# Threshold attention and a tanh-shrink layer pair: scores one slot further ahead, one slot more before the weights, and a v load in three parts

## The chip, the cores and the metric

The kernel runs on one core of one Trainium2 chip. The time is the device time of an execution in microseconds. Of the kernel before there are three executions: 511.3, 513.72 and 514.99 us, so its median is 513.72 us. One further execution was profiled: it took 509.47 us, and the span between its first and last recorded instruction is 507.7 us.

## The reference

Eight batches of eight heads have 576 rows of 64 numbers for q, k and v. What is computed is an attention that keeps only scores near the maximum of their row, followed by two dense layers:

```python
scores = scale * np.matmul(q, k.transpose(0, 1, 3, 2))
thresh = np.max(scores, axis=-1, keepdims=True) - tau
scores = np.where(scores >= thresh, scores, -1000000000.0)
attn = np.exp(scores - np.max(scores, axis=-1, keepdims=True))
attn = attn / (np.sum(attn, axis=-1, keepdims=True) + 1e-09)
x = np.matmul(attn, v)            # then heads side by side: 4608 x 512
h = x @ w_in                      # w_in 512 x 2048
g = h - np.tanh(h)
out = g @ w_out                   # w_out 2048 x 512
```

## The kernel before, in words

**Tiles.** Two heads form a pair; there are 32 pairs, four to a batch. A pair has nine score tiles of 128 query rows by 576 keys: four for each head, and a ninth ("shared") that holds the last 64 rows of both. So there are 288 tiles. Tiles go in twos, A (even number) and B (odd).

**Slots.** The order is written out by hand. One loop over a slot number `s` (L820) issues in each slot one tile's step of every stage:

- `scores(s + AHEAD)` (L373): matmuls of turned q against turned k, hi and lo halves (`kT` and a half-swapped copy `kS`), into PSUM; then VectorE copies the scores out and takes the row's maximum (L406). `AHEAD` is 8. The two shared tiles between an even and an odd pair are scored in one slot, and the slot before that scores none.
- `kink` of tile `s + MASK` (L425): ScalarE masks the scores into `z` (L433). `MASK` is 5. For pairs from 6 on, SyncE then issues a DMA that transposes a `z` of two tiles into `zT` (L440); for earlier pairs TensorE does this.
- `weights` of tile `s` (L442): ScalarE takes the exponential, from `zT` (L469) for pairs from 6 on. For the first 36 tiles this is done four slots earlier (L815).
- `attend` of tile `s - LAG` (L474): TensorE multiplies the weights with v. `LAG` is 2. `norm` divides on VectorE, and `emit_x` (L537) transposes a finished pair into the layers' input.

**Layers.** After each batch of attention a block of layer steps is started (L822 to L824), and a string of 36 letters per block (`PATTERN`, L622) says in which of the next 36 slots an "h" step (`hidden`, four matmuls of 512 columns, L565) or a "y" step (`project`, a quarter of an output tile, L591) is issued. `bend` puts tanh on ScalarE (L578), `shrink` the subtraction on VectorE (L584). What is left after the last tile runs as a tail.

**Preparation.** `plan` (from L743) lists for each pair at how many slots ahead of its first score it is loaded, split and turned. Pairs from 8 on: the loads (`load_part`, L143) are issued from ScalarE's queue, k in one DMA, q in two, v in two (128 KB and 160 KB). GpSimd splits k and q into hi and lo halves (`split`, L225 to L229), SyncE issues a transposing DMA for each (`turn`, L301), GpSimd makes `kS` from `kT` in two copies (`swap`, L323) and casts v (`split_v`, L258 to L263). The slots are the numbers in `LATER` (L746): "k0", "q0", "q1", "v0", "v1" are load parts, "ks", "qs", "vs" splits, "kt", "qt" turns, "kw" the swap. Pairs 1 to 7 take theirs from `PREP` and `k_lead`. The tags of turned k, q and kS have two buffers each (`qk_pool`, L114).

**Queues.** Each engine works in program order. ScalarE's queue holds the loads of pairs from 8 on between its activations; SyncE's queue holds all transposing DMAs and the output stores. In the built program every DMA of both queues signals one of eight completion semaphores, taken in turn, and is issued only when the DMA eight places before it, which used the same one, is complete.

```python
        at = i - 4 if i < HPAIR * TPP else i
        atts.setdefault(at + LAG, []).append(i)
        if i < NTILE:
            wts.setdefault(at, []).append(i)
            kinks.setdefault(i // 2 * 2 + 2 - AHEAD if i < 4 else i - MASK, []).append(i)
```

Of the kernel before, what the change touches and what calls it, by code (L numbers as in the profile page):

```python
# [9 lines left out]
F32 = mybir.dt.float32  # L10
# [8 lines left out]
def kernel(  # L19
# [12 lines left out]
    P = 128  # L32

    B, H, S, D = q.shape
# [11 lines left out]
    HPAIR = H // 2  # L46
# [5 lines left out]
    TPP = 9  # L52
# [7 lines left out]

    W = 2 * S

    AHEAD = 8
    LDK = 16
    MASK = 5
    LAG = 2


# [30 lines left out]
    for i in range(6):  # L99
# [8 lines left out]
    pool = lambda name, bufs, **kw: ctx.enter_context(  # L108
        tc.tile_pool(name=name, bufs=bufs, **kw)
    )  # L110
    PSUM = bass.MemoryType.PSUM
    raw_pool = pool("raw", 2)
    hl_pool = pool("hl", 2)
    qk_pool = pool("qk", 2)  # L114
    sc_pool = pool("sc", AHEAD - MASK + 2)
    st_pool = pool("st", 12)
    z_pool = pool("z", 4)
# [16 lines left out]
    raws = {}  # L134
    DUAL = 8
    AT_ONCE = 1
    LOADER = nc.scalar

    boths = {}

    def load_part(p, t, part):  # L143


        b, h0 = p // HPAIR, 2 * (p % HPAIR)
        if part == 0:
            both = raw_pool.tile([P, 2, 10, D], F32, name=f"{t}raw", tag=t)
            both = boths[t] = both[:, 0:AT_ONCE, :, :]
            for a in range(AT_ONCE):  # L150
                raws[p + a, t] = both[:, a, :, :]
        both = boths[t]
        rows = {"k": k, "q": q, "v": v}[t][b, h0 : h0 + 2 * AT_ONCE, :, :]
        heads = both.rearrange("p a (h c) d -> p (a h) (c d)", h=2)
        if t == "k":
            dst = both[:, :, 0:TPP, :].rearrange("p a c d -> p a (c d)")
            rows = rows.rearrange("(a h) s d -> a (h s) d", h=2).rearrange(
                "a (p c) d -> p a (c d)", c=TPP
            )
        elif t == "v":  # L160
            rows = rows.rearrange("h (p c) d -> p h (c d)", c=TPP)
            if part == 0:
                dst, rows = heads[0:64, :, 0 : 4 * D], rows[:, :, 0 : 4 * D]
            else:
                dst, rows = heads[64:P, :, :], rows[:, :, 4 * D :]
        elif part == 0:
            dst = heads[:, :, 0 : 4 * D]
            rows = rows[:, 0:512, :].rearrange("h (p c) d -> p h (c d)", c=4)
        else:
            dst = both[:, part - 1, 4, :]  # L170
            rows = rows[2 * part - 2 : 2 * part, 512:S, :].rearrange("h s d -> s h d")
        LOADER.dma_start(out=dst, in_=rows)

    def load(p, t):
        b, h0 = p // HPAIR, 2 * (p % HPAIR)
        hs = slice(h0, h0 + 2)
        src = {"k": k, "q": q, "v": v}[t]
        eng = nc.sync
        r = raw_pool.tile([P, 2, 10, D], F32, name=f"{t}raw", tag=t)[:, 0, :, :]
        raws[p, t] = r  # L180
        eng.dma_start(
            out=r.rearrange("p (h c) d -> p h (c d)", h=2)[:, :, 0 : 4 * D],
            in_=src[b, hs, 0:512, :].rearrange("h (p c) d -> p h (c d)", c=4),
        )
        rem = src[b, hs, 512:S, :].rearrange("h s d -> s h d")
        if t == "v":
            eng.dma_start(out=r[0:64, 4:10:5, :], in_=rem)
        else:
            eng.dma_start(out=r[:, 4, :], in_=rem)

    def load_first(t, h, eng):

        src = {"k": k, "q": q}[t]
        if (0, t) not in raws:
            raws[0, t] = raw_pool.tile([P, 2, 10, D], F32, name=f"{t}raw", tag=t)[:, 0, :, :]
        r = raws[0, t]
        if h is None:
            rem = src[0, 0:2, 512:S, :].rearrange("h s d -> s h d")
            eng.dma_start(out=r[:, 4, :], in_=rem)
        else:  # L200
            eng.dma_start(
                out=r[:, 5 * h : 5 * h + 4, :].rearrange("p c d -> p (c d)"),
                in_=src[0, h, 0:512, :].rearrange("(p c) d -> p (c d)", c=4),
            )
# [72 lines left out]
    def turn_chunk(out, c, lhsT, mixed=True):  # L277
        rhs = ident_f16
        if c == 4 and mixed:
            out, rhs = in_heads(out), by_head(rhs)  # L280
        nc.tensor.matmul(
            out=out, lhsT=lhsT, rhs=rhs, is_transpose=True, start=True, stop=True
        )

    def k_lead(p):
        if p < HPAIR + 2:
            return 6 if p in (2, 4) or p == HPAIR + 1 else 5 - (p == 1)
        return (6, 6)[1 - p % 2]
# [29 lines left out]
    def swap(p):  # L318
        m = mats[p, "k"]
        sw = qk_tile("ks")  # L320
        for lo, hi in ((0, D), (D, 0)):
            o, i = sw[lo : lo + D, 0:W], m[hi : hi + D, 0:W]
            nc.gpsimd.tensor_copy(out=o, in_=i)  # L323
        mats[p, "ks"] = sw
# [264 lines left out]
    def project(m, ms, part, ps, last, cols=slice(0, d_model)):  # L589
# [31 lines left out]

    PATTERN = lambda m: {  # L622
        0: '-h--h-hh--h-hh-h-hh-h--hh-h--hh-y-yy',
        B - 2: 'hyhyhyhyhyhyhyhyhyhyhyhyhyhyhyhy',
    }.get(m, 'h-yhyhhyhyyhyyhh-yhhyhhy-yhyyh-yyhhy')

    FIRST = 3
    quarters = lambda m: [(m, ms, part) for ms in range(4) for part in range(4)]
# [90 lines left out]
    def w_load(piece):  # L719
# [6 lines left out]
        else:  # L726
# [18 lines left out]

    LATER = {  # L746
        0: (
            ("k0", 17), ("q0", 15), ("v0", 13), ("kt", 7), ("q1", 15),
            ("ks", 8), ("v1", 12), ("vs", 6), ("qs", 10), ("qt", 7),
            ("kw", 3),  # L750
        ),
        1: (
            ("k0", 19), ("v1", 14), ("q0", 18), ("v0", 16), ("qs", 11),
            ("q1", 17), ("qt", 8), ("ks", 13), ("vs", 6), ("kt", 10),
            ("kw", 7),
        ),
    }
    for p in range(DUAL, NPAIR):
        first = TPP * p - AHEAD
        at = lambda d, f: plan.setdefault(first - d, []).append(f)  # L760
        for what, d in LATER[p % 2]:
            t, w = what
            f = {
                "0": lambda p=p, t=t: load_part(p, t, 0),
                "1": lambda p=p, t=t: load_part(p, t, 1),
                "2": lambda p=p, t=t: load_part(p, t, 2),
                "s": lambda p=p, t=t: split_v(p) if t == "v" else split(p, t),
                "t": lambda p=p, t=t: turn(p, t),
                "w": lambda p=p, t=t: swap(p) if k_by_dma(p) else None,
            }[w]  # L770
            at(d, f)
    for p in range(1, DUAL):
        first = TPP * p - AHEAD
        for d, f in PREP[3 if p == 1 else 0 :]:
            d -= p == 1 and d == 3
            if p > HPAIR and d >= LDK - 2:
                d = ((16, 14, 12), (17, 15, 13))[1 - p % 2][LDK - d]
            elif d in (7, 8) and q_by_dma(p):
                d = ((9, 9) if d == 7 else (10, 10))[1 - p % 2]
            elif d == 4:  # L780
                d = 4
            elif d == 5:
                d = k_lead(p)
            elif p in (2, 4):
                d = {8: 9, 7: 8}.get(d, d)
            plan.setdefault(first - d, []).append(lambda p=p, f=f: f(p))
        d = (6, 7)[1 - p % 2] if q_by_dma(p) else 3 - (p == 1 or p >= 5)
        d = 4 if p in (2, 4) else d
        plan.setdefault(first - d, []).append(lambda p=p: turn(p, "q"))

    load(0, "v")
# [8 lines left out]
        load(1, t)  # L800
    pieces = w_pieces()
    load_when = [3, 8, 13, 18, 21, 25, 29, 34, 38, 42, 46, 49, 52, 55, 58, 61]
    cast_when = [11, 19, 27] + [4 * i + 32 for i in range(3)] + [3 * i + 44 for i in range(10)]

    todo, stage = [], 0
    fold = const.tile([P, 64], BF16, name="fold")
# [1 line left out]
    for at in sorted(plan):  # L808
        if at < -AHEAD:
            plan.setdefault(-AHEAD, []).extend(plan.pop(at))  # L810


    kinks, wts, atts = {}, {}, {}
    for i in range(NTILE + 3):
        at = i - 4 if i < HPAIR * TPP else i  # L815
        atts.setdefault(at + LAG, []).append(i)
        if i < NTILE:
            wts.setdefault(at, []).append(i)
            kinks.setdefault(i // 2 * 2 + 2 - AHEAD if i < 4 else i - MASK, []).append(i)
    for s in range(-AHEAD, NTILE + LAG + 3):  # L820
        p, j = divmod(max(s, 0), TPP)
# [43 lines left out]
                emit_x(pp - 1)  # L865
        for step in plan.pop(s, []):
            step()
        if s + AHEAD in cast_when:
            w_cast()
        if s + AHEAD in load_when:  # L870
            w_load(next(pieces))

    for _, step in todo:
# [16 lines left out]
    _ = bass_utils  # L890
# [35 lines left out]
```

## Time and profile before

| what | value |
|---|---|
| median of three executions | 513.72 us (511.3 to 514.99) |
| profiled execution, and its span | 509.47 us, 507.7 us |
| TensorE (PE) busy | 484.1 us, 95% |
| ScalarE (ACT) busy | 432.7 us, 85% |
| VectorE (DVE) busy | 400.0 us, 79% |
| GpSimd (POOL) busy | 291.1 us, 57% |
| DMA | 95.61 MB, mean 188 GB/s |

Busy time is a sum over the span, and the stages differ: attention alone at first, then attention with layers, then layers alone from about 437 us. So the stretches matter more than the totals. "L396" names a line of the kernel; "kS<-kT" a tile written from a tile; ACTq and SPq are the queues of ScalarE and SyncE, where a DMA is issued. A wait line reads: engine, its line, who released it, total us, times, longest.

### The profile page before, as it was taken

The page shows a single profiled execution, that of the slowest core. Times are in us where ns is not written, and L with a number is a line of the kernel's source. Part 1 is how long each engine was busy: PE and PEld are TensorE (multiplying, and loading weights), DVE is VectorE, ACT ScalarE, POOL GpSimd, SP SyncE. Part 2 cuts the span into 40 slices and gives each one's busy share as a digit, 9 for nine tenths or more (in the row PEclk, how much of TensorE's full clock was granted, in tenths as well). Part 3 has the DMA queues.
Part 4 walks back from the last instruction along what each step waited for, and adds up shares of the span by engine and source line. Part 5 has one row for each costly group of instructions (what it writes and reads, how often), then busy time and mean ns, then how long its engine had stood idle before and what let it go on. Part 6 is the DMA issues. An engine that isn't in the chain of part 4 may idle for free.

```text
span 507.7 us, 12146 instructions
## 1 busy us (share of the span) xinstructions
PE 484.1 (95%) x4274; PEld 270.4 (53%) x4336; DVE 400.0 (79%) x1149; ACT 432.7 (85%) x617; POOL 291.1 (57%) x390
## 2 busy tenths in 40 slices
PE   8999899888999999999999999999998999999997
PEld 4667566444555555555555555555554555544444
DVE  5899979976989898988898889889887887544440
ACT  5999999988999999999999999999998999533430
POOL 7999999967676657574757575575567500000000
PEclk9999999998999999999999999999999999999999
DMA  6852658999999999999999999999999976211013
GB/s 198 264 163 90 196 176 220 226 189 220 211 245 228 242 227 223 242 249 211 228 228 268 216 228 228 223 231 231 212 220 252 197 131 113 76 41 43 24 40 83
DMA packets 234525, 95.61 MB, mean 188 GB/s; under 512 B 205152, under 2 KB 223840, under 8 KB 234464
## 3 DMA queue, kind: packets, MB, share of 16 engines
q1 hardware_dynamic: 213520, 73.17, 74.7%
q10 hardware_dynamic: 20944, 21.67, 15.7%
q8 instruction: 34, 0.56, 0.5%
q14 instruction: 27, 0.22, 0.1%
HBM read 36.70 MB, written 9.44 MB: 91 GB/s over the span
## 4 chain that ended last, share of the span: by engine, by line
PE 61%; POOL 12%; DMA 10%; ACT 6%; issue 5%; DVE 3%; ACTq 1%; SPq 0%; POOLq 0%
PE psY L591 20%; PE psH L565 16%; PE psS L396 14%; PE psO L499 4%; DMA zT<-z 3%; POOL kS L323 3%; PE psHt L565 3%; ACT pT L469 3%; ACT z L433 2%; DMA kT<-khl 2%; DMA kraw<-in_k_dram 2%; PE psS L387 2%; ACT th L578 1%; POOL w_in_sb L717 1%; DMA qraw<-in_q_dram 1%
## 5 line engine op out<-in xcount | busy, mean ns | idle before, releaser
L406 DVE TENSOR_SCALAR_CACHE_REDUCE sc<-psS 128x576 f32<-128x576 f32 x288 | 213.2, 752 | 28.7 <-PE psS L396 14.2
L433 ACT ACTIVATE z<-sc,nb 128x576 bf16<-128x576 f32 x288 | 217.2, 770 | 13.5 <-DVE nb L418 9.4
L591 PE MATMUL psY<-w_out_sb,g 128*128 128x512 bf16 (+1 forms) x564 | 141.5, 375 | 1.7 <-DVE nb L418 0.2
L469 ACT ACTIVATE pT<-zT 128x1152 f16<-128x1152 bf16 x117 | 135.0, 1154 | 4.6 <-DMA zT<-z 4.6
L565 PE MATMUL psH<-xT,w_in_sb 128*128 128x512 bf16 x448 | 118.8, 379 | 5.3 <-DVE g L584 2.2
L323 POOL COPY kS<-kT 64x1152 f16<-64x1152 f16 x62 | 70.7, 1141 | 74.6 <-DMA kT<-khl 55.2
L584 DVE SCALAR_TENSOR_TENSOR g<-th,psH 128x512 bf16<-128x512 f32 x128 | 87.6, 684 | 28.9 <-ACT th L578 28.1
L396 PE MATMUL psS<-kT,qT 128*128 128x512 f16 (+1 forms) x512 | 104.8, 286 | 3.3 <-DVE sc L406 1.5
L396 PE MATMUL psS<-kS,qT 128*128 128x512 f16 (+1 forms) x512 | 104.9, 287 | 0.1
L396 PEld LDWEIGHTS <-qT 128*128 128x128 f16 x1024 | 72.8, 98 | 58.6 <-issue 4.2
L578 ACT ACTIVATE th<-psH 128x512 f32<-128x512 f32 x128 | 74.6, 583 | 20.9 <-PE psH L565 20.9
L591 PEld LDWEIGHTS <-g 128*128 128x128 bf16 x592 | 51.3, 98 | 55.1 <-issue 1.1
L565 PEld LDWEIGHTS <-w_in_sb 128*128 128x128 bf16 x576 | 49.0, 98 | 57.3 <-issue 5.5
L499 PE MATMUL psO<-vb,pT 128*128 128x65 bf16 x1024 | 53.6, 195 | 0.0
L499 PEld LDWEIGHTS <-pT 128*128 128x128 f16 x1024 | 44.5, 98 | 9.9
L229 POOL TENSOR_TENSOR qhl<-qraw,qhl 128x576 f16<-128x576 f32 x31 | 39.7, 1281 | 2.6
L229 POOL TENSOR_TENSOR khl<-kraw,khl 128x576 f16<-128x576 f32 x31 | 39.7, 1280 | 2.6
L461 ACT ACTIVATE pT<-psZ 128x512 f16<-128x512 bf16 (+1 forms) x54 | 35.1, 653 | 2.5 <-PE psZ L452 2.3
L225 POOL TENSOR_SCALAR qraw<-qraw 128x576 f32<-128x576 f32 x31 | 20.8, 670 | 20.9 <-DMA qraw<-in_q_dram 19.6
L603 DVE COPY yo<-psY 128x512 f32<-128x512 f32 (+1 forms) x31 | 21.1, 680 | 13.3 <-PE psY L591 12.4
L492 PE MATMUL psO<-vb,pT 128*128 128x130 bf16 x128 | 28.3, 221 | 2.1 <-ACT pT L469 1.8
L525 DVE TENSOR_TENSOR osb<-psO,rc 128x256 bf16<-128x256 f32 x64 | 27.2, 425 | 2.2
(77 smaller groups left out, 448.6 us busy)
## 6 DMA issues: line engine op xcount, KB each, us to landing
out_dram<-yo SPq DMA_DIRECT2D x32, 256.0 KB, 2.9
kraw<-in_k_dram ACTq DMA_DIRECT2D x24, 288.0 KB, 4.2
qraw<-in_q_dram ACTq DMA_DIRECT2D x24, 256.0 KB, 4.1
wt<-in_moe_w_in_dram SPq DMA_DIRECT2D x8, 512.0 KB, 4.6
wt<-in_moe_w_out_dram SPq DMA_DIRECT2D x8, 512.0 KB, 4.2
vraw<-in_v_dram ACTq DMA_DIRECT2D x24, 160.0 KB, 4.0
vraw<-in_v_dram ACTq DMA_DIRECT2D x24, 128.0 KB, 4.2
vraw<-in_v_dram SPq DMA_DIRECT2D x8, 256.0 KB, 3.6
```

The source lines that it names most:

```text
L229: nc.gpsimd.tensor_tensor(out=hl[:, :, 1, :], in0=x, in1=hl[:, :, 0, :], op=ALU.subtract)
L323: nc.gpsimd.tensor_copy(out=o, in_=i)
L396: nc.tensor.matmul(out=ps[:, dst], lhsT=lhs, rhs=cols(p, kk, hh), start=(n == 0), stop=(n == 1),)
L406: nc.vector.tensor_scalar(out=sc, in0=ps[:, lo : lo + S], scalar1=SC, scalar2=None, op0=ALU.mult, op1=ALU.max, accum_out=mx[:, c : c + 1],)
L433: nc.scalar.activation(out=z, in_=sc, func=ACT.Prelu, bias=nb, scale=1.0, alpha=STEEP)
L461: nc.scalar.activation(out=pt[:, off * P : (off + n) * P], in_=ps[:, 0 : n * P], func=ACT.Exp)
L469: nc.scalar.activation(out=pt[:, 0 : n * P], in_=zts.pop(i)[:, 0:n, :], func=ACT.Exp)
L499: nc.tensor.matmul(out=po[:, t - 1 + ab, :], lhsT=pt[:, blk * P : (blk + 1) * P], rhs=vb[:, hh, c, :], start=False, stop=(n == 7), skip_gr ...
L565: nc.tensor.matmul(out=ps, lhsT=w_in_sb[:, c, n * P : (n + 1) * P], rhs=xs[m][:, c, :] if m < B else xR[:, c, :, :], start=(c == 0), stop= ...
L578: nc.scalar.activation(out=th, in_=ps, func=ACT.Tanh)
L584: nc.vector.scalar_tensor_tensor(out=gs[m][:, n, :], in0=th, scalar=-1.0, in1=ps, op0=ALU.mult, op1=ALU.add,)
L591: nc.tensor.matmul(out=ps, lhsT=gs[m][:, n, ms * P : (ms + 1) * P], rhs=w_out_sb[:, n, cols], start=(n == 0), stop=(n == DF_C - 1),)
```

## The change

`AHEAD` becomes 9 and `MASK` 6: scores and mask of a tile are issued one slot earlier against its weights. The table `SOONER` moves weights and attend of the tiles of pairs 0 to 3 five slots forward instead of four, and of pairs 4 and 5 one slot instead of none, so that for pairs 0 to 5 the distance from score to mask, weights and attend is what it was. From pair 6 on, mask and weights stand six slots apart instead of five. Attend follows the weights by two slots as before.

`qk_pool` gets three buffers. The v load becomes three DMAs, 128, 128 and 32 KB, from ScalarE's queue (24 more DMAs in all). `LATER` has other slots; pairs 8 and 9 have tables of their own. `LEADS` lists the slots of pairs 1 to 7; against the first score of the pair they are the former ones, but for pair 5, whose k is turned one slot later. Two layer patterns change: the one of the second block, and the one used where none is named. Blocks begin at the same slot as before, which is now one score later. `raw_pool` tiles lose a half that was never used. `cast_when` is the same list written out.

```diff
-    AHEAD = 8
+    AHEAD = 9
     LDK = 16
-    MASK = 5
+    MASK = 6
...
-    qk_pool = pool("qk", 2)
+    qk_pool = pool("qk", 3)
...
+    V_PARTS = ((0, 0, 4), (64, 4, 8), (64, 8, 9))
...
-            both = raw_pool.tile([P, 2, 10, D], F32, name=f"{t}raw", tag=t)
-            both = boths[t] = both[:, 0:AT_ONCE, :, :]
+            both = raw_pool.tile([P, AT_ONCE, 10, D], F32, name=f"{t}raw", tag=t)
+            boths[t] = both
...
-            if part == 0:
-                dst, rows = heads[0:64, :, 0 : 4 * D], rows[:, :, 0 : 4 * D]
-            else:
-                dst, rows = heads[64:P, :, :], rows[:, :, 4 * D :]
+            at, c0, c1 = V_PARTS[part]
+            dst = heads[at : at + 64, :, c0 % 4 * D : (c1 - c0 + c0 % 4) * D]
+            if c0 == 8:
+                dst = heads[at : at + 64, :, 4 * D : 5 * D]
+            rows = rows[:, :, c0 * D : c1 * D]
...
+    LEADS = {
+        1: (8, 7, 4, 4, 2),
+        2: (9, 8, 6, 4, 4),
+        3: (8, 7, 5, 4, 3),
+        4: (9, 8, 6, 4, 4),
+        5: (8, 7, 5, 4, 2),
+        6: (8, 7, 6, 4, 2),
+        7: (8, 7, 6, 4, 2),
+    }
...
     PATTERN = lambda m: {
         0: '-h--h-hh--h-hh-h-hh-h--hh-h--hh-y-yy',
+        1: '-hyhyhhyhyyhyhhh-yhhyhhy-hyyyy-yyhyh',
         B - 2: 'hyhyhyhyhyhyhyhyhyhyhyhyhyhyhyhy',
-    }.get(m, 'h-yhyhhyhyyhyyhh-yhhyhhy-yhyyh-yyhhy')
+    }.get(m, 'h-yhyh-yhyyhyhhyhyhhhyhyyh-yyh-yyhhy')
...
     LATER = {
         0: (
-            ("k0", 17), ("q0", 15), ("v0", 13), ("kt", 7), ("q1", 15),
-            ("ks", 8), ("v1", 12), ("vs", 6), ("qs", 10), ("qt", 7),
-            ("kw", 3),
+            ("k0", 17), ("q0", 17), ("v0", 13), ("kt", 7), ("q1", 15),
+            ("ks", 8), ("v1", 12), ("v2", 12), ("vs", 5), ("qs", 12),
+            ("qt", 7), ("kw", 2),
         ),
         1: (
-            ("k0", 19), ("v1", 14), ("q0", 18), ("v0", 16), ("qs", 11),
-            ("q1", 17), ("qt", 8), ("ks", 13), ("vs", 6), ("kt", 10),
-            ("kw", 7),
+            ("k0", 19), ("v1", 14), ("v2", 12), ("q0", 18), ("v0", 16),
+            ("qs", 13), ("q1", 17), ("qt", 8), ("ks", 14), ("vs", 5),
+            ("kt", 10), ("kw", 7),
+        ),
+    }
+    FIRST_LATER = {
+        8: (
+            ("k0", 17), ("q0", 15), ("v0", 13), ("kt", 7), ("q1", 15),
+            ("ks", 9), ("v1", 12), ("v2", 12), ("vs", 6), ("qs", 10),
+            ("qt", 7), ("kw", 3),
+        ),
+        9: (
+            ("k0", 18), ("v1", 15), ("v2", 15), ("q0", 18), ("v0", 16),
+            ("qs", 10), ("q1", 17), ("qt", 8), ("ks", 13), ("vs", 6),
+            ("kt", 11), ("kw", 7),
         ),
     }
...
-        for what, d in LATER[p % 2]:
+        for what, d in FIRST_LATER.get(p) or LATER[p % 2]:
...
+    SOONER = (5, 5, 5, 5, 1, 1, 0)
     kinks, wts, atts = {}, {}, {}
     for i in range(NTILE + 3):
-        at = i - 4 if i < HPAIR * TPP else i
+        at = i - SOONER[min(i // TPP, 6)]
```

More of the change, by code (lines that the diff above doesn't have):

```diff
@@ L178, in load @@
         eng = nc.sync
-        r = raw_pool.tile([P, 2, 10, D], F32, name=f"{t}raw", tag=t)[:, 0, :, :]
+        r = raw_pool.tile([P, AT_ONCE, 10, D], F32, name=f"{t}raw", tag=t)[:, 0, :, :]
         raws[p, t] = r
@@ L194, in load_first @@
         if (0, t) not in raws:
-            raws[0, t] = raw_pool.tile([P, 2, 10, D], F32, name=f"{t}raw", tag=t)[:, 0, :, :]
+            raws[0, t] = raw_pool.tile([P, AT_ONCE, 10, D], F32, name=f"{t}raw", tag=t)[:, 0, :, :]
         r = raws[0, t]
@@ L779 @@
                 d = ((9, 9) if d == 7 else (10, 10))[1 - p % 2]
+            elif p in LEADS and d in (8, 7, 5, 4):
+                d = LEADS[p][(8, 7, 5, 4).index(d)]
             elif d == 4:
@@ L787 @@
         d = (6, 7)[1 - p % 2] if q_by_dma(p) else 3 - (p == 1 or p >= 5)
-        d = 4 if p in (2, 4) else d
+        d = LEADS[p][4] if p in LEADS else d
         plan.setdefault(first - d, []).append(lambda p=p: turn(p, "q"))
@@ L802 @@
     load_when = [3, 8, 13, 18, 21, 25, 29, 34, 38, 42, 46, 49, 52, 55, 58, 61]
-    cast_when = [11, 19, 27] + [4 * i + 32 for i in range(3)] + [3 * i + 44 for i in range(10)]
+    cast_when = [11, 19, 27, 32, 36, 40, 44, 47, 50, 53, 56, 59, 62, 65, 68, 71]
     todo, stage = [], 0
@@ L867 @@
             step()
-        if s + AHEAD in cast_when:
+        for _ in range(cast_when.count(s + AHEAD)):
             w_cast()
-        if s + AHEAD in load_when:
+        for _ in range(load_when.count(s + AHEAD)):
             w_load(next(pieces))
```

## The prediction

> **What bounds the kernel now.** I read the page's slices first, then the busy time in stretches of 12.5 us, then the waits, then the timeline around the largest wait.
>
> ```profile
> PE   8999899888999999999999999999998999999997
> ACT  5999999988999999999999999999998999533430
> POOL 7999999967676657574757575575567500000000
> PEclk9999999998999999999999999999999999999999
> ```
>
> TensorE is full nearly everywhere. The ninth to tenth slices (100 to 127 us) stand out: PE falls to 8, and its clock falls there and nowhere else. GpSimd is full only at the start. The stretches (columns: length, then busy us of PE, PEld, DVE, ACT, POOL, clock, DMA share, GB/s) give sizes:
>
> ```profile
> 37.50:50.00 12.50, 12.05 (x174) 8.73 (x173) 11.42 (x36) 12.34 (x21) 11.69 (x17) 1.00 0.29 92
> ...
> 100.00:112.50 12.50, 10.15 (x90) 5.69 (x90) 9.85 (x32) 11.50 (x17) 7.77 (x9) 1.00 1.22 205
> 112.50:125.00 12.50, 10.21 (x94) 5.51 (x94) 7.72 (x24) 10.16 (x15) 10.02 (x15) 0.86 1.21 198
> ...
> 200.00:212.50 12.50, 12.39 (x108) 6.81 (x109) 11.92 (x36) 12.10 (x18) 7.88 (x10) 1.00 1.24 246
> ...
> 325.00:337.50 12.50, 11.59 (x116) 6.42 (x116) 9.62 (x31) 10.78 (x16) 9.37 (x14) 1.00 1.31 238
> ...
> 387.50:400.00 12.50, 11.28 (x97) 6.20 (x98) 10.55 (x29) 11.77 (x18) 8.40 (x11) 1.00 1.18 214
> ```
>
> From 125 us on, PE works 12.3 to 12.4 of 12.5 us, and ACT 12.1: PE is the bound and ACT stands close behind it. Two stretches drop out, 325 and 387. The whole span holds 507.7 - 484.1 = 23.6 us of idle PE. Who ends those waits:
>
> ```profile
> POOL kS L323 <- DMA kT<-khl: 55.2, 18, 4.7
> ...
> ACT pT L469 <- DMA zT<-z: 4.6, 5, 2.0
> ...
> PE psO L492 <- ACT pT L469: 1.8, 1, 1.8
> ```
>
> The longest line costs nothing by itself: GpSimd waits ahead of its next work, and `kS` is ready 1.5 us or more ahead of the first score in every pair from 9 on (pair 28 has least, pair 11 most, 9.1 us). The second and third are the ones that stop PE. The largest, on ACT's timeline:
>
> ```profile
> 112.87 0.58 ACT L578 ACTIVATE th<-psH 128x512 f32<-128x512 f32 x1
> 114.37 0.60 ACTq L172 DMA_DIRECT2D vraw<-in_v_dram  x1
> 115.02 0.78 ACT L433 ACTIVATE z<-sc,nb 128x576 bf16<-128x576 f32 x1 [1.57 <-DVE sc L406]
> 115.70 0.58 ACT L578 ACTIVATE th<-psH 128x512 f32<-128x512 f32 x1
> 116.18 1.15 ACT L469 ACTIVATE pT<-zT 128x1152 f16<-128x1152 bf16 x1
> ```
>
> The releaser named there had long been done: ACT stands from 113.45 to 114.37 before a v load. That load shares its completion semaphore with the q turn of pair 9, issued at 106.37, which took 8.0 us to land, until 114.35. Weights come late, PE waits 1.81 us for them (until 117.39), and the clock trace shows half clock from 117.39 for 3.41 us.
>
> **What the Trainium skill says.** "TensorE: Matmul & The Clock Gate", Part 1, "What's actually happening": after an idle window of about 3.4 us the array's clock is halved for at least a window. This trace agrees: one window of 3.41 us at 0.50, right after the wait. "Perfetto Trace Analysis", "DMA Instruction — HWDGE (DVE, Sync)": a DMA's recorded start is when its semaphores are satisfied, so a stop on one shows as a gap before it; the 0.92 us gap fits. "DMA: Bandwidth & Descriptors", "Issuing engines are not separate DMA queues": loads from one queue and transposes from another interleave on the same 16 engines. Here `zT` lands in 3.4 us where nothing collides and in 7.0 us (issued 324.27) where the q turn and q and v loads are in flight.
>
> **The change part by part.** A slot in the steady stage is 52.9 us per block of 36, 1.47 us.
>
> *One slot more for `zT`.* ACT's five waits on `zT` sum to 4.6 us, the longest 2.03. Each shrinks by up to 1.47, so at most 0.6 stays and 4.0 us of ACT time come free. What PE gets of it I read from PE: the stretch at 325 is 12.39 - 11.59 = 0.8 short of its neighbours, that at 387 is 12.35 - 11.28 = 1.1 short, and after the 0.89 us wait at 102.3 PE stands 0.91 us before an h step at 104.49. Together 2.8 us. Next to be late there is ACT itself, full around each, so I take no more.
>
> *The stop at 115 us.* The load and its partner stay eight apart, so the stop of 1.57 us probably stays. The attend that waited is now issued one slot later, after a y step (0.86) and a score tile (0.49): 1.35 us of PE work go before it, against one more mask on ACT (0.67 net of overlap), so PE gains 0.7. ACT also comes there 0.89 us less late. 1.81 - 0.7 - 0.9 leaves 0.2: 1.6 us saved. If PE stays busy the clock stays full: half of 3.41, 1.7 us. Sum 3.3. From below it is zero (both PE and ACT are shifted alike), from above 3.5.
>
> *Three buffers.* SyncE waits 9.6 us on the scores' matmuls before turning k or q; that goes. But SyncE waits 190 us on ACT's `z` and its neighbours anyway, so I count 0 (0 to 1 us gained).
>
> *Order of preparation.* On SyncE the order of all transposes is the same in the built programs except near the end; only the stores move by one. On GpSimd, for even pairs from 10 on, the swap now stands behind the odd pair's q split (2.76 us from first to last instruction). Putting that split ahead, at the later of its data and the k split before it, delays the swap by 2.3 us at pair 14, 1.5 at pair 30 and at most 1.0 elsewhere; slack there was 3.4 and 4.4 us, so 1.1 us remains. Cost 0; if that cover is gone, each microsecond of lateness is one of PE, on 11 pairs. Earlier q loads and splits only add slack.
>
> *Third v DMA.* 24 issues of about 0.57 us, the duration of q's 32 KB part. The existing 0.6 us issues run beside an activation and leave no gap after them in 300 us of steady stage, so 0.1 to 0.2 us in all for descriptors. The dear part is the ring of eight semaphores: with 27 DMAs per two pairs instead of 25, the partner is nearer. Counting slots between a load on ACT and its partner in the built programs, from score 120 to 260: 8 of 76 are four slots or fewer (5.9 us) apart before, 23 of 90 after. Most DMAs land in 3.3 to 5 us. Taken 0.7; bounds 0 and 15 x 1.0, minus what ACT can absorb (below).
>
> *One slot of run-in, and the patterns.* Blocks start one score later; PE's idle share at 62 to 90 us is 7% of a slot of 1.4 us: 0.1. The patterns keep the counts of h and y. Three h steps in a row (slots 18 to 20) ask for a PSUM buffer freed one slot earlier: 0 to 0.3 us in each of five blocks; taken 0.2. Against this the steady stage has 0.65 us of idle per block to be won; taken 0. Pair 5's k turn one slot later: GpSimd's order is unchanged, 0, with 0.3 either way.
>
> Sum: -2.8 - 3.3 + 0.2 + 0.7 + 0.1 + 0.2 = -4.9 us. From the profiled 509.47 that is 504.6; the runs' median is 4.25 above it, and the same 4.9 gives 508.8. I say 509.0, -0.9%.
>
> **The rivals.** *Only the small waits go* (chance 0.28): PE and ACT are moved alike, the stop at 115 and the half clock stay. Then -2.8 + 1.2 = -1.6: 512.1. For it: the distance from weights to attend is still two slots. Against: the extra y step.
>
> *The ring of eight stops ACT* (0.18). ACT is an engine that computes, so a load that waits for a transpose holds all masks behind it, and PE's scores and weights after that. The 15 further tight loads (score 120 to 260; some 20 over the whole) at 1.0 us, between the 0.4 us gap at 93 us and the 1.57 at 113, make 20 us; ACT absorbs 0.34 us per pair (52.89 - 51.54 in pairs 10 to 13, over four), 22 pairs: 7.5. Left 12.5; the waits that the slot removes return as well, so only 3.3 - 0.4 is gained: +9.6, 523.3. It decides from (7.5 + 2.9) / 20 = 0.5 us per tight load. Against: at five slots and fewer before, 300 us show no such stop.
>
> *The slower executions had more of the same* (0.21). What they spend beyond the profiled one is not shown. If it is late transposes, and half of the 4.25 us goes too: 506.9. Against: nothing in the profile says so.
>
> *A third thing was the limit* (0.03): DMA rate, a share of 1.15 to 1.24 throughout; transposes would only queue longer, and the time stays at 513.7.
>
> **How the numbers follow.** First case 0.30, 509.0, from 507 to 511. The rest as above. About 1% (5.1 us) is what a measurement of this kernel tells from no change. Faster by over 1%, below 508.6: nearly all of the 506.9 case, close to half of the first, little of the second: 0.37. Slower by over 1%, above 518.9: most of the ring's case, 0.17. The rest is 0.46. The range of 503.5 to 519 takes in the first, second and fourth cases with their unknowns, down to the whole 4.25 us and a little more, and leaves out most of the ring's case: somewhat under 2 in 10.
>
> **What would show it.** Right: ACT's wait on `zT` under 1.5 us in all; PE above 11 us in 100 to 112.5 and in 112.5 to 125; no half clock near 117 us; stretches from 300 to 400 us all at 12.2 or more. Wrong: gaps on ACT before L172-type loads of v or q, sum over 3 us (the ring); GpSimd swaps of even pairs ending after the first score wants them; a steady block longer than 52.9 us (the patterns).

## The result and the profile after

The changed kernel takes 528.57 us (median of four executions, 528.17 to 529.24); the kernel before, on the same chip, takes 514.36 us (511.3 to 517.43). The ratio is 1.028, with an interval of 1.024 to 1.033: the change makes the kernel slower, by 14.2 us. The prediction was 509.0, faster. The profiled execution took 529.24 us with a span of 527.0 us, 19.3 us more than the span before. Ratios here and below leave out the executions of a kernel that took over 1.5% longer than its fastest one, so a ratio can differ from that of the two medians; where that matters for the reading, both are given.

The slices of the page after, the same four rows as were read before:

```profile
PE   8999899589999999898979988999999999999997
ACT  5999998779989997998979979999798999643330
POOL 8999999578466657475574748483948510000000
PEclk9999999979999999999999999999999999999999
```

Before, TensorE (PE) was full nearly everywhere from the eleventh slice on; now it has a hole at the eighth (92 to 105 us) and falls to 7 or 8 at irregular places. ScalarE (ACT) is low in the same places or next to them. PE's recorded idle time grew by 10.6 us (from 23.6 to 34.2) and its busy time by 8.7 us (484.1 to 492.8). Part of this is the record itself. Of the 4336 matmuls the trace of before lacks 62, all of layer steps, and the trace of after lacks none. Taking 62 such records out of the trace of after lowers its busy time by 3 to 4 us, so the real idle time before was nearer 20 us than the 23.6 that the prediction read. Another 1.7 us of busy time, by estimate, is half of the 3.4 us for which the half clock lasts longer. The rest was not explained.

The stretches (length, then busy us of PE, PEld, DVE, ACT, POOL, clock, DMA share, GB/s), for the windows shown before, and 262.5 in addition:

```profile
37.50:50.00 12.50, 12.05 (x178) 8.79 (x176) 11.42 (x36) 12.34 (x21) 11.69 (x17) 1.00 0.30 92
...
100.00:112.50 12.50, 8.48 (x47) 3.83 (x47) 6.97 (x21) 8.84 (x12) 7.42 (x8) 0.74 1.29 183
112.50:125.00 12.50, 11.89 (x118) 6.50 (x117) 11.34 (x36) 12.27 (x17) 8.87 (x14) 0.99 0.93 213
200.00:212.50 12.50, 10.45 (x103) 5.76 (x101) 8.68 (x27) 9.34 (x14) 8.37 (x12) 1.00 1.24 199
262.50:275.00 12.50, 9.34 (x82) 5.02 (x80) 8.39 (x26) 8.76 (x13) 9.18 (x12) 1.00 1.20 199
325.00:337.50 12.50, 11.13 (x98) 6.06 (x97) 10.92 (x31) 12.22 (x18) 6.83 (x7) 1.00 1.30 220
387.50:400.00 12.50, 12.50 (x114) 6.99 (x112) 11.46 (x34) 12.11 (x17) 3.98 (x7) 1.00 1.14 212
```

At 37.5 us nothing changed. At 112.5 and 387.5 PE is as busy as was forecast (11.89 and 12.50). But at 200 us PE had 12.39 and ACT 12.10 before, and now 10.45 and 9.34: both engines stand. The DMA share there is the same 1.24, while the bytes moved fell from 246 to 199 GB/s.

The waits after (engine, line, releaser: total us, times, longest):

```profile
POOL kS L337 <- DMA kT<-khl: 69.9, 15, 7.7
...
PE psH L579 <- DVE g L598: 11.8, 10, 3.2
...
ACT z L447 <- DMA zT<-z: 7.4, 3, 3.7
...
PE psS L410 <- POOL kS L337: 4.3, 5, 1.3
ACT pT L483 <- DMA zT<-z: 4.2, 5, 1.3
PE psS L410 <- DMA qT<-qhl: 4.1, 3, 2.1
...
ACT z L447 <- DMA qraw<-in_q_dram: 3.2, 1, 3.2
```

ACT's masks (`z`, L447) seem to wait for transposes and loads. They read neither: a mask needs a score tile. What stands ahead of them in ACT's queue is a load. The timeline of ACT, SyncE's queue (SPq) and ACT's own queue (ACTq) around the largest such gap:

```profile
258.54 9.17 SPq L454 DMA_TRANSPOSE zT<-z  x3
258.93 0.34 ACTq L175 DMA_DIRECT2D kraw<-in_k_dram  x1
...
261.55 0.39 ACTq L175 DMA_DIRECT2D qraw<-in_q_dram  x1
...
263.45 1.16 ACT L483 ACTIVATE pT<-zT 128x1152 f16<-128x1152 bf16 x1
267.73 0.58 ACTq L175 DMA_DIRECT2D qraw<-in_q_dram  x1
...
268.35 0.78 ACT L447 ACTIVATE z<-sc,nb 128x576 bf16<-128x576 f32 x1 [3.74 <-DMA zT<-z]
```

ACT ends an activation at 264.61 and issues the next load at 267.73. Eight places before that load in the program's order of DMAs stands the first `zT` of the top line, issued at 258.54; the trace has it landing at 267.71. With it in flight were two more `zT`, the k load of 288 KB and the q load of 256 KB, and all of these took 7.7 to 9.7 us to land. In the kernel before, the corresponding loads and transposes (247.78 to 252.74 us) took 4.5 to 6.7 us, and no load waited.

The landing times of all of them (size, median us) fit. After, then before:

```profile
kraw<-in_k_dram ACTq DMA_DIRECT2D x24, 288.0 KB, 4.8
qraw<-in_q_dram ACTq DMA_DIRECT2D x24, 256.0 KB, 5.5
...
zT<-z SPq DMA_TRANSPOSE x117, 5.0
```

```profile
kraw<-in_k_dram ACTq DMA_DIRECT2D x24, 288.0 KB, 4.2
qraw<-in_q_dram ACTq DMA_DIRECT2D x24, 256.0 KB, 4.1
...
zT<-z SPq DMA_TRANSPOSE x117, 4.4
```

From each trace I took, for every load of pairs from 8 on, the time between the end of the instruction before it and its start. After, ten loads stop ACT for more than 0.15 us, for 13.1 us together. At every one of them, the DMA that used the same completion semaphore before lands 0.02 to 0.10 us ahead of the load's start: eight times a `zT` that took 6.0 to 9.2 us, and near 95 us a k and a q load that took 6.7 and 8.5. Before, there was one such stop, of 0.93 us. In the kernels of the next section that issue their loads from ACT there are 52 more stops, and each ends in the same way, within 0.10 us of that landing. So the wait for the semaphore is shown, stop by stop.

A wider count takes ACT's whole idle time, in gaps over 0.15 us, between two activations that have such a load between them. This is 24.8 us after, in 21 gaps, and 2.4 us before, in three. It is called ACT's idle time at loads below. It grew by 22.4 us where the span grew by 19.3, but that is no proof of the size: the experiments show that the two do not go together one for one.

PE's largest wait after, `psH` on `g`, could also come from the new layer patterns. Six of its gaps are over 0.5 us and hold 10.6 of PE's 12.1 us of idle time before `psH`. Five of them begin 0.3 to 2.5 us after one of the ten stops ends (the sixth, of 1.4 us, 10.9 us after one), so they mostly follow from ACT's stops: a late `th` makes a late `g`.

### The profile page after: what moved, and what is told of

Same layout as the page of the kernel before. It is cut to its first block, busy times and chain, and to the rows that moved or that the text cites. A ratio compares the mean times of both kernels' runs of the same rounds, so it can differ in the third digit from the quotient of the medians.

```text
span 527.0 us, 12155 instructions
## 1 busy us (share of the span) xinstructions
PE 492.8 (94%) x4336; PEld 273.0 (52%) x4336; DVE 403.4 (77%) x1149; ACT 432.6 (82%) x617; POOL 291.2 (55%) x390
## 4 chain that ended last, share of the span: by engine, by line
PE 46%; DMA 18%; POOL 13%; ACT 9%; issue 5%; DVE 5%; ACTq 2%; SPq 1%; POOLq 0%; DVEq 0%
PE psY L605 15%; PE psH L579 12%; PE psS L410 10%; DMA zT<-z 7%; DMA kraw<-in_k_dram 4%; ACT z L447 4%; DMA qraw<-in_q_dram 4%; DMA kT<-khl 3%; PE psHt L579 3%; ACT pT L483 3%; PE psO L513 2%; ACTq L175 2%; DVE g L598 2%; POOL kS L337 2%; ACT th L592 2%
## 5 line engine op out<-in xcount | busy, mean ns | idle before, releaser
L447 ACT ACTIVATE z<-sc,nb 128x576 bf16<-128x576 f32 x288 | 215.9, 772 | 26.6 <-DMA zT<-z 7.4
L605 PE MATMUL psY<-w_out_sb,g 128*128 128x512 bf16 (+1 forms) x592 | 145.8, 373 | 0.0
L579 PE MATMUL psH<-xT,w_in_sb 128*128 128x512 bf16 x480 | 125.0, 383 | 12.3 <-DVE g L598 11.8
L410 PEld LDWEIGHTS <-qT 128*128 128x128 f16 x1024 | 73.3, 98 | 69.9 <-issue 11.6
L579 PEld LDWEIGHTS <-w_in_sb 128*128 128x128 bf16 x576 | 50.2, 98 | 69.3 <-issue 16.0
L617 DVE COPY yo<-psY 128x512 f32<-128x512 f32 (+1 forms) x31 | 21.1, 680 | 13.1 <-PE psY L605 12.4
```

Source lines behind the costliest of these rows:

```text
L410: nc.tensor.matmul(out=ps[:, dst], lhsT=lhs, rhs=cols(p, kk, hh), start=(n == 0), stop=(n == 1),)
L447: nc.scalar.activation(out=z, in_=sc, func=ACT.Prelu, bias=nb, scale=1.0, alpha=STEEP)
L579: nc.tensor.matmul(out=ps, lhsT=w_in_sb[:, c, n * P : (n + 1) * P], rhs=xs[m][:, c, :] if m < B else xR[:, c, :, :], start=(c == 0), stop= ...
L605: nc.tensor.matmul(out=ps, lhsT=gs[m][:, n, ms * P : (ms + 1) * P], rhs=w_out_sb[:, n, cols], start=(n == 0), stop=(n == DF_C - 1),)
```

## The experiments

The theory after the result has two parts. *The ring*: a load on ACT's queue may not be issued before the DMA eight places back has landed, and more DMAs per pair move that one nearer. *The bunching*: the new slots put loads and transposes on top of one another, so that each lands later. The rival is that something else cost the time (patterns, late swaps or bytes), and that the stops only show it.

Every ratio below is against the kernel before on the same chip, on which its median was 516.79, 517.11 or 514.95 us. Its single executions spread from 508.65 to 523.74, so that differences under about 1% are seldom told apart. In the counts from the built programs, "close partner" means that the DMA eight places back was issued four slots or less before the load, counted from score 120 to 260.

**Two v DMAs in the changed kernel.** `V_PARTS` and the entries "v2" are taken out, all else stays.

```diff
-            at, c0, c1 = V_PARTS[part]
...
+            if part == 0:
+                dst, rows = heads[0:64, :, 0 : 4 * D], rows[:, :, 0 : 4 * D]
+            else:
+                dst, rows = heads[64:P, :, :], rows[:, :, 4 * D :]
```

> The kernel after, but with v in two DMAs again (128 and 160 KB) and the third part's slots dropped; all else stays. Ring theory (a load on ScalarE's queue may start only when the DMA eight places before it has landed, and the third v DMA brings that partner nearer): tight loads fall from 23 of 90 to 11 of 75, ACT's stops go, 510 to 517 us. Slots theory (k and q loads bunched, swap behind the q split): no change, 526 to 530. Scores-ahead or layer-pattern theory: no change, 526 to 530.

Measured: 524.65 us, ratio 1.022 (1.011 to 1.034), between the forecasts of the theories. By the ratios 0.6% of the 2.8% came back, by the medians of all executions (1.015 here, 1.028 for the change) 1.2%. In the built program the loads with a partner four slots or less back fell from 23 of 90 to 11 of 75, but the q loads still take 5.9 us, and ACT is still idle at loads for 18.1 us. The close partners alone do not explain the result.

**Three v DMAs in the kernel before.** The reverse: only the v load is changed.

```diff
+            at, c0, c1 = ((0, 0, 4), (64, 4, 8), (64, 8, 9))[part]
...
-            ("ks", 8), ("v1", 12), ("vs", 6), ("qs", 10), ("qt", 7),
+            ("ks", 8), ("v1", 12), ("v2", 12), ("vs", 6), ("qs", 10), ("qt", 7),
...
-            ("k0", 19), ("v1", 14), ("q0", 18), ("v0", 16), ("qs", 11),
+            ("k0", 19), ("v1", 14), ("v2", 12), ("q0", 18), ("v0", 16), ("qs", 11),
```

> The kernel before with only the v load in three DMAs (128, 128 and 32 KB), the third at slot 12. Ring theory: tight loads rise from 8 of 76 to 25 of 91, 519 to 529 us. Slots theory and scores-ahead theory: nothing of theirs is in it, 512 to 517.

Measured: 520.43 us, ratio 1.017 (1.007 to 1.027). The bytes are the same, and the price is 1.7%; by the medians of all executions it is 0.7%, so its size is not well known. All four executions lie above the median of before, and all but one above every execution of before. ACT's idle time at loads rose from 2.4 to 16.4 us and its idle time before activations that read `zT` from 4.6 to 10.1 us. Is it the issue on ACT, the smaller transfers, or the place in the ring?

**A DMA of 1 KB per pair in the kernel before, on SyncE's queue.** It reads sixteen rows of v that nobody uses; nothing is added on ACT.

```diff
+    def tiny(p):
+        one = tiny_pool.tile([16, 16], F32, name="one", tag="one")
+        nc.sync.dma_start(out=one, in_=v[p // HPAIR, 0, 0:16, 0:16])
...
+        at(12, lambda p=p: tiny(p))
```

> The kernel before with one more DMA of 1 KB (16 rows of 64 bytes) per pair from 8 on, issued from SyncE's queue at slot 12, into a tile that nothing reads. It adds places in the ring of eight but no load on ScalarE's queue and hardly any bytes. Ring theory: tight loads on ACT 19 of 76, 517 to 527 us. If the third v DMA costs by its issue on ScalarE or by its descriptors: 512 to 516. Slots theory: 512 to 516.

Measured: 521.47 us, ratio 1.019 (1.006 to 1.031); 0.9% by the medians. Within the error, twenty-four DMAs of 1 KB cost as much as 24 more v loads of 32 KB. The place where the time shows differs: ACT is idle at loads for 2.0 us only, and waits for late transposes instead (its waits, then those of the kernel with three v DMAs above):

```profile
ACT pT L474 <- DMA zT<-z: 16.9, 19, 3.4
```

```profile
ACT pT L470 <- DMA zT<-z: 8.7, 8, 3.4
```

So these two sizes cost alike, which speaks for the place in the queues and against the bytes. The profiles fit a loss that is passed to whichever queue has to wait: at a load ACT stands itself, at a transpose SyncE stands and ACT waits for `zT`. The run does not tell a place in the ring from a place in SyncE's own queue, since the small DMA has both. That the v DMA on ACT's queue costs about the same speaks for the ring.

**Loads from SyncE's queue in the changed kernel.**

```diff
-    LOADER = nc.scalar
+    LOADER = nc.sync
```

> The kernel after with the loads of pairs from 8 on issued from SyncE's queue instead of ScalarE's. The ring is as tight, but what it stops is SyncE, not an engine that computes. Ring theory with the stop on ACT as the cost: ACT has no gaps before loads; 510 to 520 us, less sure since loads and transposes then stand behind each other. Slots theory: bunched loads in front of transposes, 526 to 540.

Measured: 552.81 us, ratio 1.079 (1.068 to 1.090); every theory had forecast 540 or less. ACT no longer stops at any load, and the kernel is much slower. The loads wait in SyncE's queue behind the transposes and the transposes behind loads:

```profile
ACT pT L483 <- DMA zT<-z: 37.0, 24, 2.6
PE psS L410 <- POOL kS L337: 24.7, 12, 3.3
...
PE psS L410 <- DMA qT<-qhl: 10.7, 7, 3.4
```

That a DMA lands late is not the cause here: in this run the median of `zT` from issue to landing is 3.6 us and that of the q loads 3.9, lower than in the kernel before. They must therefore be issued late.

**Loads from GpSimd's queue, in both kernels.** GpSimd's DMAs use other semaphores: in the built program the DMA that a transpose has to wait for is then 9.6 slots back on average, not 5.4.

```diff
-    LOADER = nc.scalar
+    LOADER = nc.gpsimd
```

> The changed kernel with its loads of k, q and v issued by GpSimd instead of ACT. In the built program they then leave the ring of eight semaphores that ACT's and SyncE's DMAs share, and a transpose on SyncE has its partner 9.6 slots back on average instead of 5.4. The bytes, their shapes and their slots stay. Theory A (the ring is what costs): ACT stops at no load, ACT's wait for zT falls under 3 us, the time is 505 to 515, ratio 0.98 to 1.00. Theory B (loads and transposes collide on the DMA engines, the ring only passes the lateness on): landing times and PE's waits for qT, kT and kS stay, 520 to 530. Theory C (GpSimd has no room: some 90 issues of about 1 us make the swaps late): PE's waits for kS rise over 8 us, 518 to 535.

> The kernel before with the same edit alone: loads from GpSimd, nothing else. It had only 2.0 us of ACT stops at loads and 4.6 us of waits for zT. Theory A: small gain, 508 to 515, and then slower than or equal to the changed kernel with the same edit, since that one also has a slot more for zT. Theory B: no difference from the kernel before, 514 to 519. Theory C: slower, 518 to 530, with late swaps.

Measured: 551.07 us for the changed kernel, ratio 1.074 (1.064 to 1.083), and 543.02 us for the kernel before, 1.059 (1.051 to 1.066). Theory A fell, theory C held, and more strongly than its numbers said. In the changed kernel 120 issues take 76 us of GpSimd (44.3 for v and 31.7 for q, k not counted), and PE's waits for `kS` reach 27.6 us in one and 16.2 us in the other. But why is `zT` late in the kernel before with this edit, for 35.2 us, when its partner in the ring is nearly twice as far away?

```profile
ACT pT L469 <- DMA zT<-z: 35.2, 19, 4.4
```

Three extracts of its timeline, of GpSimd, of SyncE's queue and of ACT:

```profile
182.19 1.28 POOL L229 TENSOR_TENSOR khl<-kraw,khl 128x576 f16<-128x576 f32 x1
```

```profile
183.49 1.68 SPq L301 DMA_TRANSPOSE kT<-khl  x1
185.27 1.40 SPq L301 DMA_TRANSPOSE qT<-qhl  x1
186.76 3.20 SPq L440 DMA_TRANSPOSE zT<-z  x2
```

```profile
190.93 1.16 ACT L469 ACTIVATE pT<-zT 128x1152 f16<-128x1152 bf16 x1 [2.51 <-DMA zT<-z]
```

SyncE, in whose queue all transposes stand, issues the k turn at 183.49, as soon as GpSimd has ended the split at 183.47. The masks' transposes stand behind it in SyncE's queue: the one of 186.76 lands at 190.85, and ACT has waited 2.51 us for it. A late split reaches ACT through SyncE's queue, without the ring. These two runs therefore do not test the ring; they show that GpSimd has no room for it, and that this third coupling exists.

**Nine slots ahead alone, in the kernel before.** `AHEAD`, `MASK` and the shift of the first pairs, nothing else.

```diff
-    AHEAD = 8
+    AHEAD = 9
...
-    MASK = 5
+    MASK = 6
...
-        at = i - 4 if i < HPAIR * TPP else i
+        at = i - (5, 5, 5, 5, 1, 1, 0)[min(i // TPP, 6)]
```

> The kernel before with only scores nine slots ahead, mask at six and the table that moves weights and attend of the first 54 tiles; patterns, load slots, two buffers and two v DMAs as before. Ring-and-bunching theory (the loss comes from DMAs that are more and nearer together, and from loads on ScalarE that wait for the DMA eight places before): loads are untouched against the scores, tight loads 4 of 76; 506 to 515 us, ACT's wait on zT under 3 us. Scores-ahead theory (the loss is in the moved weights and the layer patterns): 520 to 529.

Measured: 517.86 us, ratio 1.001 (0.995 to 1.007), between the two forecasts. The part of the change from which the prediction took its gain gives nothing. Its waits:

```profile
PE psS L396 <- POOL kS L323: 4.4, 4, 1.3
...
ACT z L433 <- DMA zT<-z: 2.8, 1, 2.8
ACT pT L469 <- DMA zT<-z: 2.0, 3, 1.1
```

The wait for `zT` did fall, from 4.6 to 2.0 us. But ACT's idle time at loads rose from 2.4 to 11.6 us and PE's wait for `kS` from 0.4 to 4.9, although fewer loads have a close partner (4 of 76, 8 before). `zT` lands in 4.9 us at the median, 4.4 before. So loads stop ACT without more DMAs or closer partners. Why its transposes land later was not found.

**Parts of the change taken back one after the other.** First the load slots: the tables of before, with v in three; then v in two as well; then the old layer patterns as well (nine slots ahead, three buffers and `LEADS` stay).

```diff
-            ("k0", 17), ("q0", 17), ("v0", 13), ("kt", 7), ("q1", 15),
-            ("ks", 8), ("v1", 12), ("v2", 12), ("vs", 5), ("qs", 12),
-            ("qt", 7), ("kw", 2),
+            ("k0", 17), ("q0", 15), ("v0", 13), ("kt", 7), ("q1", 15),
+            ("ks", 8), ("v1", 12), ("v2", 12), ("vs", 6), ("qs", 10), ("qt", 7),
+            ("kw", 3),
...
+    FIRST_LATER = {}
```

> The kernel after, v in three DMAs, but with the load, split and swap slots of before (q of even pairs at 15, swap at 3, no tables of their own for pairs 8 and 9; the third v part at 12). Ring theory alone: tight loads 23 of 90 as in the kernel after, stays at 524 to 530. Bunching theory (k, q and the q turn at one slot make latencies of 6 to 9 us): 517 to 523. Swap theory (kS late behind the q split): PE's wait on kS under 1 us, 515 to 524.

> The kernel after with both undone: v in two DMAs and the load slots of before. What stays are nine slots ahead, six to the mask, three buffers, the tables for pairs 1 to 7 and the new layer patterns. Ring-and-bunching theory: 505 to 515 us, ACT stops at loads under 4 us. Pattern theory (h steps in a row wait for their PSUM buffer): 518 to 526, with PE's wait of psH on g at 6 us or more.

```diff
-        1: '-hyhyhhyhyyhyhhh-yhhyhhy-hyyyy-yyhyh',
...
-    }.get(m, 'h-yhyh-yhyyhyhhyhyhhhyhyyh-yyh-yyhhy')
+    }.get(m, 'h-yhyhhyhyyhyyhh-yhhyhhy-yhyyh-yyhhy')
```

> The changed kernel with v in two DMAs and the old load slots (the run that lay 0.8% above the kernel before), and now with the old patterns of layer steps too; nine slots ahead, three buffers and the other k and q turns of pairs 1 to 7 stay. With the old patterns the built program has 4 of 76 loads with a partner four slots or less back, with the new ones 11. If patterns (by PSUM buffers or through the order of the DMAs) made the 0.8%: 513 to 517, ratio 0.995 to 1.003. If the third buffer or the turns of pairs 1 to 7 made it: 518 to 522, ratio 1.005 to 1.01.

Measured: 524.75 us, 518.96 us and 517.03 us. The first lies in the range of the ring alone and not in that of the bunching. The second misses the range of the two together (505 to 515 us), with ACT idle at loads for 13.2 us instead of under 4; PE's wait of `psH` on `g` is 3.7 us and not the 6 of the pattern theory. The third lies between its two ranges. With the run above they make a chain from the kernel before to the changed one:

| kernel | ratio (interval) | step | step by medians | ACT idle at loads | ACT idle before zT's readers | PE waits for kS | for kT, qT | before psH |
|---|---|---|---|---|---|---|---|---|
| before | 1 | | | 2.4 | 4.6 | 0.4 | 3.7 | 4.2 |
| + nine ahead | 1.001 (0.995 to 1.007) | +0.1% | +0.1% | 11.6 | 2.0 | 4.9 | 6.3 | 2.9 |
| + three buffers, LEADS | 1.005 (1.002 to 1.009) | +0.4% | +0.3% | 15.3 | 0.0 | 3.9 | 4.7 | 2.2 |
| + patterns | 1.008 (1.005 to 1.011) | +0.3% | 0.0% | 13.2 | 3.4 | 4.6 | 4.1 | 4.2 |
| + v in three | 1.013 (0.998 to 1.028) | +0.5% | +1.1% | 22.4 | 1.8 | 2.0 | 9.0 | 6.9 |
| + slots = changed | 1.028 (1.024 to 1.033) | +1.6% | +1.3% | 24.8 | 4.2 | 4.3 | 8.3 | 12.1 |

(us of the profiled executions; the PE columns are PE's idle time before instructions that use kS, kT or qT, or write psH, gaps over 0.1 us.) Neighbouring intervals overlap, so no step is told from nothing by itself; the slots and the third v DMA are the largest by either count. Old and new patterns differ by 0.3%, 1.3 us, which is not told from nothing.

**The q load alone, both ways.** Of the slots, the first q load of even pairs is moved from 15 to 17 slots ahead, to the slot of its k load. Once it is moved in the kernel before, alone; once it is put back in the changed kernel, alone.

```diff
-            ("k0", 17), ("q0", 15), ("v0", 13), ("kt", 7), ("q1", 15),
+            ("k0", 17), ("q0", 17), ("v0", 13), ("kt", 7), ("q1", 15),
```

> The kernel before with one number changed: the first q part of even pairs from 10 on at slot 17 instead of 15, beside that pair's k load and the odd pair's q turn (pair 8 too). Bunching theory: median landing of q loads rises from 4.1 to 5 us or more, ACT stops at loads of 5 us or more, 518 to 526 us. If only the third v DMA matters: 512 to 517.

> The changed kernel with one entry put back: the first q load of even pairs 15 slots ahead, as before, instead of 17; v stays in three DMAs and all else stays. The count of close partners stays (23 of 90 loads, as in the changed kernel). If the ring's distances alone set the loss: no difference from the changed kernel, 525 to 530. If it is the bunching of the q load with the k load and the odd pair's q turn: 517 to 522, with q loads landing in about 4.5 us instead of 5.5.

Measured: in the kernel before, 522.57 us (511.36 to 527.22), ratio 1.002 (0.996 to 1.008). This ratio rests on 4 of the 20 executions; the medians of all 20 and of the 47 of the kernel before differ by 1.1%. So whether the entry costs time there is left open. Its profiled execution, of 521.6 us, has the forecast landing time of the q loads, 5.8 us, but not the forecast stops: ACT is idle at loads for 0.6 us, and waits for `zT` instead.

```profile
ACT pT L469 <- DMA zT<-z: 21.8, 17, 4.3
```

The entry is also not free of the ring: moved in the kernel before, it raises the close partners from 8 to 12.

Put back in the changed kernel, 522.32 us (518.61 to 525.82), ratio 1.019 (1.011 to 1.027) instead of 1.028 (1.024 to 1.033), intervals that overlap a little; the medians differ by 1.3%. Here close partners are the same 23 of 90, and loads and transposes land nearly as soon as in the kernel before:

```profile
kraw<-in_k_dram ACTq DMA_DIRECT2D x24, 288.0 KB, 4.4
qraw<-in_q_dram ACTq DMA_DIRECT2D x24, 256.0 KB, 4.5
...
zT<-z SPq DMA_TRANSPOSE x117, 4.5
```

ACT's wait for `zT` falls from 4.2 to 0.6 us and PE's idle time before psH from 12.1 to 7.6; ACT's idle time at loads stays (24.9 us). So in the changed kernel this one entry of the table is worth some 1%. The count of close partners is not what changed, and the landing times are; that they carry the gain is the likely reading, from one profile of each kernel.

The same pair of kernels shows that ACT's idle time at loads is no price list. With the entry back it is as long as in the changed kernel, and the span is 6.9 us shorter. Against the kernel before, the span of the kernels in the chain grew by half to nearly all of what this idle time grew by (12.9 and 6.7 us with three buffers, 22.4 and 19.3 in the changed kernel).

None of these kernels is faster than the kernel before.

## Why the prediction was wrong

The prediction had the main mechanism among its rivals, as "*The ring of eight stops ACT*" with a chance of 0.18 and 523.3 us, and it took 0.7 us for it in its own sum. Two of its costs failed, and neither of its two gains came.

*"Third v DMA ... Taken 0.7; bounds 0 and 15 x 1.0"* is a mis-sized term. The rule (a load on ACT holds up masks) and the count of close partners (23 of 90) were right. The size came from the kernel before, where one stop was seen in 300 us. But one more DMA per pair there costs 1.7% as a v load and 1.9% as 1 KB on SyncE's queue, that is 8.9 and 9.7 us on its 517 us; by the medians, 3.6 and 4.7 us. On the changed kernel the third v DMA costs 3 to 6 us (0.6% by the ratios, 1.2% by the medians), where ACT stops with two as well. The rival's sum assumed 20 stops of 1.0 us, of which ACT would absorb 7.5 us. There were ten, of 1.3 us on average and up to 3.1, in an idle time at loads of 24.8 us. How much of it ACT absorbs differs from kernel to kernel, from nearly nothing to about half. That the rival's 523.3 us is nearer to 528.57 than 509.0 is therefore in part luck: its number and size of stops were both off, and it left out the next step.

*"Earlier q loads and splits only add slack"* is the step that was false in kind. Moving a load earlier is safe for its own data. It also puts 256 KB on the DMA engines beside the k load and the `zT` transposes: q loads took 5.5 us instead of 4.1, `zT` 5.0 instead of 4.4. A transpose that lands late is late for ACT, and the load eight places later is late too. One entry put back returns about 1 of the 2.8%. The prediction counted the moved load's issue, and not the time for which its bytes are in the others' way. It had its own example on the page: `zT` in 3.4 us alone and 7.0 us with loads in flight. The earlier splits were not tested alone.

Its other steps:

- *"One slot more for zT": -2.8.* The waits went, as it said (4.6 us before, 0.0 to 3.4 in the four kernels between), and the time did not: 1.001 with this edit alone. It asked what would be late next and answered "ACT itself, full around each". It was ACT, but stopped at loads, not full: its idle time at loads is 11.6 us there.
- *"The stop at 115 us": -3.3.* The stretch from 112.5 us is better, 11.89 of 12.5 us with the clock at 0.99. The large stop is now 20 us earlier, at 95.1 and 97.3 us:

```profile
93.66 1.15 ACT L483 ACTIVATE pT<-zT 128x1152 f16<-128x1152 bf16 x1
95.14 2.80 ACTq L175 DMA_DIRECT2D vraw<-in_v_dram  x2
97.99 0.77 ACT L447 ACTIVATE z<-sc,nb 128x576 bf16<-128x576 f32 x1 [3.19 <-DMA qraw<-in_q_dram]
```

  Two v loads wait there for a k load (issued 88.39, 6.73 us) and a q load (88.86, 8.45 us). PE stands, and the half clock lasts 6.83 us instead of 3.41 (from 105.99). Tiles 54 to 107, by VectorE's copies of their scores, take 90.3 us instead of 84.0. With nine slots ahead alone a load stops ACT here too (at 95.86 us, for 3.0 us), and they take 86.7, so part of this comes with the gain that was sought. On the clock, the prediction's "This trace agrees" holds for the halving and the 3.41 us; the idle time ahead of it was 1.81 us, shorter than the window that it quotes.
- *"Three buffers": 0.* Together with `LEADS` +0.4%, with intervals that overlap; not told from 0, and the two were not tested apart.
- *"Order of preparation": 0, with 1.1 us of cover.* PE's waits for kS rose from 0.4 to 4.3 us. But they are 3.9 to 4.9 us in three kernels with the old slots of swaps too, and 2.0 in a fourth, so the swap's new place is not shown to be their cause. Its costing was neither confirmed nor refuted.
- *"One slot of run-in, and the patterns": +0.3.* +1.3 us for the patterns in the chain, within its error.
- *"A third thing was the limit"*, the DMA rate: nothing supports it. The bytes moved per second fell in the stretch at 200 us (246 to 199 GB/s), and 1 KB costs about as much as 32.

Its list of signs named the right one: gaps on ACT before loads, "sum over 3 us (the ring)". They sum to 13.1 us. The steady stage shows it as long odd pairs: pairs 15, 17 and 19 take 15.9, 15.2 and 17.1 us from the copy of their first score to that of the next pair's, 13.0 before.

What stays open is how the 2.8% divides. The third v DMA and the q entry, each taken out of the changed kernel alone, return 0.6 and 1.0% by the ratios and 1.2 and 1.3% by the medians; together that is a little over half, or nearly all. Small parts below half a per cent are hidden by the executions' own spread. And why the transposes land later with nine slots ahead alone, without more DMAs, was not settled.

## What to carry to other kernels

When a computing engine's queue also issues DMAs, count the DMAs between each load and the one whose semaphore it takes over, and take the slack as the smallest distance against the longest landing time, not the median. One more DMA per pair cost time here, at 1 KB as at 32 KB. When a load is moved earlier, ask which transfers it now lies beside: their landing time is what someone else's queue waits for. An absence of stops in one profile does not price the next DMA.

## What the runs showed that was not expected

- A DMA of 1 KB per pair (24 in all) costs 1.9% (0.6 to 3.1; 0.9 by the medians), about as much as 24 loads of 32 KB on ACT's queue.
- All 63 stops of ACT at a load over 0.15 us, in ten kernels, end within 0.10 us after the landing of the DMA that used the same semaphore before, whatever releaser the profile names for the next activation.
- Moving loads away from the engine that they stop is worse: +7.9% from SyncE's queue and +7.4% from GpSimd's, against +2.8% with the stops. In the first, DMAs land faster (`zT` 3.6 us) and the waits for them are still longer, so they are issued later.
- On GpSimd's queue a load's issue takes 0.62 to 0.66 us of GpSimd's own time, shown as busy: 72 of v are 44.3 us, 48 of q 31.7.
- In the changed kernel SyncE's issue of a `zT` transpose, 1.45 us at the median, lasts up to 4.60 us, with loads and other transposes in flight (the one at 263.11 us).
